# Attention and a low-rank mixer on one core: the first batch's query, key and value handling is reordered

## The chip, the core and the metric

The kernel runs on one core of a Trainium2 chip. Five engines work beside each other, each through its own instructions in order: TensorE (PE in the profile; its weight loads are PEld), VectorE (DVE), ScalarE (ACT), GpSimd (POOL) and SyncE (SP). SyncE only issues transfers; GpSimd issues transfers too, and computes. Sixteen DMA engines carry all transfers. An instruction that waits holds up everything behind it on its engine. The metric is device microseconds from start to end of one execution, and lower is better.

## What is computed

Four batches, eight heads, 768 positions, head dimension 64. First attention with a local window of 96 and 8 global keys, a bias that falls with distance, and a softmax. Then, over the heads' outputs put side by side (512 columns), a low-rank mix over positions and a two-layer feed-forward with residual:

```python
scores = scale * q @ k.T
rel = pos[:, None] - pos[None, :]
keep = (pos[None, :] < 8) | ((rel >= 0) & (rel < 96))
scores = where(keep, scores - slope[h] * dist, -1e9)
x = softmax(scores) @ v            # heads side by side: [4, 768, 512]
u = x + (U @ V applied over positions of x)
out = u + relu(u @ w_ch1) @ w_ch2  # 512 -> 2048 -> 512
```

## The kernel before

**Tiling.** Work goes by pairs of heads: a batch has `NP` = 4 pairs, so pair 0 to 3 are batch 0 and pairs 4 to 15 the others. Positions lie in six blocks of 128. Since the window is below 128, a block of queries needs only its own block of keys and the one before, in which the 8 global keys are put in place of the first positions. Scores are made transposed, keys on partitions: 1408 columns for a head, in three chunks of 512, 512 and 384.

**Steps of a pair i.**
- `load_qk(i)`: two transfers from SyncE's queue, 393 KB each, into staging tiles `qst` and `kst` with three buffers each (L86 to L96). `cast_qk`: a cast of each to 16 bits (L102), on VectorE for pairs 0 and 1, on GpSimd for the others.
- `load_v(i)`: from GpSimd's queue, one transfer a head, with a cast to 16 bits, into one of four buffers `vbuf` (L110). Each row moved is 64 numbers long.
- `st_T(i)`: twelve transposes on TensorE (L223) into two PSUM tiles, then copies to SBUF: the query half of head 0 by ScalarE (L229), keys kT by VectorE (L230), kA, which is the previous block's keys with the global keys put in (L231, L232), and the query half of head 1 by VectorE (L235).
- `st_A(i)`: vA, the same for v: one copy on GpSimd (L241), then the global rows on VectorE (L242).
- Scores: batch 0 uses `st_SE(i, c)`, in which TensorE adds the bias by a matmul of a scaled identity `slI` with a table `rel16` (L258), then the score matmuls (L263, L268), and ScalarE takes the exp straight from PSUM (L281). Later batches use `st_S` (the bias is added by VectorE from a table `relcat`, L294) and `st_E` (exp, L302).
- `st_V(i, hi)`: 11 matmuls a head (L314, L318) whose 65th column is the sum of the weights; VectorE normalises (L323, L325) and GpSimd casts the result to `x16` (L328).
- `st_M1(i)`: six matmuls with U (L336) and a copy of the result, `tmp` (L340). `st_M2(i)`: matmuls with V and an identity (L347, L352) that give `uT`, transposed, copied by VectorE and ScalarE (L358, L360).
- When all four pairs of a batch are through M2, `queue_ff` makes its feed-forward: units of four matmuls `hps` with W1 (L376) and a relu (L380, into `htr`, two buffers), and units of four matmuls with W2 (L389, L395), then the output (L401, L402). `fill(n)` puts n units of the batch before between the steps of later pairs.

**What sets the order.** Batch 0 has no feed-forward work beside it. Its order is written out by hand, within `tc.manual_schedule()`, up to `ordered.close()`: per engine the instructions stand as the code names them, though a scheduler may put instructions of the part behind it between them. In the loop over pairs (L428 on) the first score chunk is followed by the M1 of two pairs ago, the V of the pair before and the casts of pair i + 2; then chunk 1, then `st_T(i + 1)` with the slopes of the next pair's two heads (L162), the next load, M2 of two pairs ago, chunk 2 and `st_A(i)`. W1 is loaded at i = 1, W2 at i = 3, v of pair i + 2 at i = 2 and 3, four transfers for each weight, all from GpSimd's queue with a cast. Behind `ordered.close()` come pairs 4 to 15, where the scheduler chooses each engine's order.

Of the kernel before, what the change touches and what calls it, by code (L numbers as in the profile page):

```python
# [11 lines left out]
FP32 = mybir.dt.float32  # L12
# [8 lines left out]
def kernel(  # L21
# [13 lines left out]
    nc = tc.nc  # L35
    B, H, S, D = q.shape
    NG = int(n_global)
    NL = int(n_local)
    P = 128
    DM = H * D  # L40
    NSB = S // P
# [41 lines left out]
    NVB = 4  # L83
    vbuf = [cst.tile([P, 2, NSB, D + 1], FP16, name=f"v16_{i}") for i in range(NVB)]

    def load_qk(i):  # L86
        b, h0 = i // NP, 2 * (i % NP)
        got = []
        for src, nm in ((q, "qst"), (k, "kst")):
            st = stp.tile([P, 2, NSB, D], FP32, name=nm, tag=nm, bufs=3)  # L90
            nc.sync.dma_start(
                st.rearrange("p h n d -> p h (n d)"),
                src[b, h0:h0 + 2].rearrange("h (p n) d -> p h (n d)", n=NSB),
            )
            got.append(st)
        staged[i] = got  # L96

    def cast_qk(i, eng):
        got = []
        for st, nm in zip(staged.pop(i), ("q16", "k16")):  # L100
            st16 = stp.tile([P, NSB, 2, D], FP16, name=nm, tag=nm, bufs=2)
            eng.tensor_copy(st16.rearrange("p n h d -> p h n d"), st)  # L102
            got.append(st16)
        cast[i] = got

    def load_v(i):
        b, h0 = i // NP, 2 * (i % NP)
        vt = vbuf[i % NVB]
        for hi in range(2):
            nc.gpsimd.dma_start(  # L110
                vt[:, hi, :, 0:D], v[b, h0 + hi].rearrange("(n p) d -> p n d", p=P)
            )
        vts[i] = vt

    NPAIR = B * NP
# [2 lines left out]

    ordered = ExitStack()
    ordered.enter_context(tc.manual_schedule())  # L120
    for i in range(3):
        load_qk(i)


# [4 lines left out]
    def warm(n):  # L129
        wps = ps_oc("warm")  # L130
        for _ in range(n):
            nc.tensor.matmul(wps, zw[:, 0:P], zw, start=True, stop=True)
# [24 lines left out]

    slI = cst.tile([P, H, P], BF16, name="slI")

    def slopes(h0, h1):  # L160
        for h in range(h0, h1):
            nc.vector.tensor_scalar_mul(slI[:, h], ident16, slope[h] / qk_scale)  # L162

    slopes(0, 2)
    for vt in vbuf:
        nc.vector.memset(vt[:, :, :, D:D + 1], 1.0)
    load_v(0)
# [15 lines left out]
    def load_uv():  # L183
        nc.gpsimd.memset(u16, 0.0)
        nc.gpsimd.dma_start(u16[:, :, 0:R], moe_U.rearrange("(c p) r -> p c r", p=P))
        nc.gpsimd.memset(v16w, 0.0)
        nc.gpsimd.dma_start(v16w[0:R], moe_V)
# [10 lines left out]
    def load_w2(c):  # L198
        nc.gpsimd.dma_start(w2_16[:, 4 * c:4 * c + 4], w2v[:, 4 * c:4 * c + 4])
# [4 lines left out]
    def new_batch(b):  # L204
        xs[b] = xp.tile([P, NSB, DM], FP32, name="x_sb", tag="x_sb", bufs=3)
        x16s[b] = xp.tile([P, NSB, DM], FP16, name="x16", tag="x16")
        tmps[b] = xp.tile([P, DM], FP16, name="tmp16", tag="tmp16", bufs=3)
        uTs[b] = xp.tile([P, NDC, S], FP16, name="uT", tag="uT")
# [4 lines left out]
    def st_T(i):  # L213
        stq, stk = cast.pop(i)
        kT = kp.tile([P, S], FP16, name="kT", tag="kT")
        kA = kp.tile([P, NSB - 1, P], FP16, name="kA", tag="kA")
        tps = []
        for st in (stq, stk):

            tp = ps_th("tp", FP16, S)  # L220
            tps.append(tp.rearrange("d (n p) -> d p n", n=NSB))
            for n in range(NSB):
                nc.tensor.matmul(  # L223
                    tp[:, n * P:(n + 1) * P], st[:, n].rearrange("s h d -> s (h d)"), ident16,
                    is_transpose=True, start=(n == 0), stop=(n == NSB - 1),
                )
        tq, tk = tps
        z = qz[i % 2]
        nc.scalar.copy(z[0][0:D].rearrange("d (p n) -> d p n", n=NSB), tq[0:D])  # L229
        nc.vector.tensor_copy(kT.rearrange("d (p n) -> d p n", n=NSB), tk)  # L230
        nc.vector.tensor_copy(kA.rearrange("d n p -> d (n p)"), kT[:, 0:S - P])  # L231
        nc.vector.tensor_copy(  # L232
            kA[:, 1:, 0:NG], kT[:, 0:NG].unsqueeze(1).broadcast_to((P, NSB - 2, NG))
        )
        nc.vector.tensor_copy(z[1][D:P].rearrange("d (p n) -> d p n", n=NSB), tq[D:P])  # L235
        kts[i], kas[i] = kT, kA

    def st_A(i):
        vt = vts[i]
        vA = vap.tile([P, 2, NSB - 1, D + 1], FP16, name="vA", tag="vA")  # L240
        nc.gpsimd.tensor_copy(vA, vt[:, :, 0:NSB - 1])  # L241
        nc.vector.tensor_copy(  # L242
            vA[0:NG, :, 1:],
            vt[0:NG, :, 0:1].broadcast_to((NG, 2, NSB - 2, D + 1)),
        )
        vas[i] = vA
# [27 lines left out]
    def st_SE(i, c):  # L274

        if c == 0:
            for hi in range(2):
                eps[i, hi] = scp.tile([P, W], FP16, name=f"ep{hi}", tag=f"ep{hi}")
        for hi in range(2):
            sc, c0, tot, _ = scores(i, hi, c, True)  # L280
            nc.scalar.activation(  # L281
                eps[i, hi][:, c0:c0 + tot], sc[:, 0:tot], AF.Exp, scale=qk_scale
            )
# [47 lines left out]
    def st_M1(i):  # L331
        b, dc = i // NP, i % NP
        ch = slice(dc * P, (dc + 1) * P)
        tps = ps_th("tmp_ps")
        for n in range(NSB):
            nc.tensor.matmul(  # L336
                tps[:, 0:P], u16[:, n], x16s[b][:, n, ch],
                start=(n == 0), stop=(n == NSB - 1),
            )
        nc.vector.tensor_copy(tmps[b][:, ch], tps[:, 0:P])  # L340

    def st_M2(i):
        b, dc = i // NP, i % NP
        ch = slice(dc * P, (dc + 1) * P)
        for g in range(2):
            ups = ps_th("ups")
            nc.tensor.matmul(  # L347
                ups[:, 0:GT], tmps[b][:, ch], v16w[:, g * GT:(g + 1) * GT],
                start=True, stop=False,
            )  # L350
            for t in range(NTG):
                nc.tensor.matmul(  # L352
                    ups[:, t * P:(t + 1) * P], x16s[b][:, NTG * g + t, ch], ident16,
                    start=False, stop=(t == NTG - 1),
                )
            dst = uTs[b][:, dc, g * GT:(g + 1) * GT]
            if g == 0:
                nc.vector.tensor_copy(dst, ups[:, 0:GT])  # L358
            else:
                nc.scalar.copy(dst, ups[:, 0:GT])  # L360
# [54 lines left out]


    new_batch(0)
    cast_qk(0, nc.vector)
    st_T(0)
    warm(2)  # L420
    cast_qk(1, nc.vector)
    load_qk(3)
    load_v(1)
    load_uv()
    nc.vector.memset(qz[1][0][D:P], 0.0)
    nc.vector.memset(qz[1][1][0:D], 0.0)
    load_v(2)
    for i in range(NP):  # L428
        st_SE(i, 0)
        if i == 0:  # L430
            cast_qk(2, nc.gpsimd)
        if i >= 2:
            st_M1(i - 2)
        else:
            warm(1)
        if i:
            st_V(i - 1, 0)
            st_V(i - 1, 1)
        if i == 0:
            load_v(3)  # L440
        if i:
            cast_qk(i + 2, nc.gpsimd)
        st_SE(i, 1)
        st_T(i + 1)
        if i < 3:
            slopes(2 * i + 2, 2 * i + 4)
        if i:
            load_qk(i + 3)
        if i >= 2:
            st_M2(i - 2)  # L450
        if i == 1:
            for c in range(4):
                load_w1(c)
        st_SE(i, 2)
        st_A(i)
        if i >= 2:
            load_v(i + 2)
        if i == 2:
            table(relcat)
        if i == 3:  # L460
            for c in range(4):
                load_w2(c)
    st_M1(NP - 2)
    st_V(NP - 1, 0)
    st_V(NP - 1, 1)
    st_M2(NP - 2)
    st_M1(NP - 1)
    st_M2(NP - 1)
    ordered.close()
    queue_ff(0, 0)  # L470
    queue_ff(0, 1)

    new_batch(1)
    for i in range(NP, NPAIR):
        b, hp = divmod(i, NP)
        if i + 3 < NPAIR:
            load_qk(i + 3)
        if i + 2 < NPAIR:
            load_v(i + 2)
        st_A(i)  # L480
        for c in range(3):
            st_S(i, c)
            fill(1)
        st_E(i, 0)
        st_E(i, 1)
        if i > NP:
            st_M2(i - 1)
            if hp == 0:
                queue_ff(b - 1, 0)
                queue_ff(b - 1, 1)  # L490
        fill(2)
        if i + 1 < NPAIR:
            if hp == NP - 1:
                new_batch(b + 1)
            st_T(i + 1)
        if i + 2 < NPAIR:
            cast_qk(i + 2, nc.gpsimd)
        fill(3)
        st_V(i, 0)
        fill(2)  # L500
        st_V(i, 1)
        fill(3)
        st_M1(i)
        fill(1)
# [39 lines left out]
```

## Time and profile before

| | us |
|---|---|
| runs of the kernel: lowest, median, highest | 280.97, 282.31, 283.50 |
| the profiled execution, span from first to last instruction | 279.8 |
| its own time beside that span | not given apart from the span; the three runs stand 1.2 to 3.7 above it |
| PE busy | 255.3 (91%) |
| DVE busy | 147.8 (53%) |
| ACT busy | 123.2 (44%) |
| POOL busy | 87.2 (31%) |
| mean granted TensorE clock | 0.963 of full |

The profile's page opens with busy time by engine, and then cuts the span into 40 slices of 7.0 us each, with one digit a slice: the busy share in tenths. Further views of the same trace are lists of instructions in order of time (start, duration, engine, line, operation, tiles, count, and in brackets the idle time before it with what ended it), a table of waits (who waited for whom: total us, times, longest), a table of busy time for chosen stretches, and transfers by queue. The queue called software_dynamic (q0) is GpSimd's, hardware_dynamic (q1) is SyncE's. In the first 70 us GpSimd's queue moved 6.06 MB in 19168 packets, and SyncE's 8.65 MB in 5984.

### The profile page before, as it was taken

To read this page: it belongs to the slowest core of one execution; us is meant where nothing else is said; L and a number is where in the kernel's file an instruction comes from. 1 tells how busy PE (TensorE), PEld (TensorE's weight loads), DVE (VectorE), ACT (ScalarE), POOL (GpSimd) and SP (SyncE) were. 2 spreads that over 40 slices of the span, in tenths; PEclk is the share of its full clock that TensorE was granted. 3 is DMA by queue.
4 is the path that set the end of the run, shared out by engine and by line. 5 is a ranking of instruction groups with operands and counts; after the bars stand their busy time and mean duration, and the time that the engine had idled before them with its cause. 6 is when DMAs were issued, how large, how long until landed. Compare 5 with 4: busy or idle time off the path is not lost.

```text
span 279.8 us, 5080 instructions
## 1 busy us (share of the span) xinstructions
PE 255.3 (91%) x2076; PEld 156.1 (56%) x2076; DVE 147.8 (53%) x301; ACT 123.2 (44%) x209; POOL 87.2 (31%) x129
## 2 busy tenths in 40 slices
PE   7765775899998999799999999999999999999994
PEld 3544554566556655566456655675566555545541
DVE  6766799156666564755957575754574440010011
ACT  2434551565218650668037630856076604604700
POOL 8948688360425124330606042300200010000000
PEclk9779896699999999999999999999999999999999
DMA  6999999992462527170634023000110021001001
GB/s 220 277 281 181 198 233 235 227 239 25 150 105 15 128 63 152 55 127 2 164 79 40 2 43 64 37 2 0 75 41 0 2 76 40 0 37 75 2 37 75
DMA packets 42327, 26.64 MB, mean 95 GB/s; under 512 B 26912, under 2 KB 39232, under 8 KB 42304
## 3 DMA queue, kind: packets, MB, share of 16 engines
q0 software_dynamic: 30144, 7.44, 27.5%
q1 hardware_dynamic: 12160, 18.88, 20.0%
q8 instruction: 16, 0.26, 0.4%
q14 instruction: 7, 0.06, 0.1%
HBM read 27.46 MB, written 6.29 MB: 121 GB/s over the span
## 4 chain that ended last, share of the span: by engine, by line
PE 62%; DVE 8%; ACT 4%; issue 2%; ACTq 0%
PE hps L376 25%; PE cps L395 24%; ACT ep L302 3%; PE tp L223 3%; DVE sp L294 2%; PE sc L268 2%; PE cps L389 2%; PE sc L263 2%; DVE qz L235 2%; DVE kT L230 2%; DVE osb L401 1%; PE tmp_ps L336 1%; PE ob L318 1%; PE ups L352 1%; PE ups L347 1%
## 5 line engine op out<-in xcount | busy, mean ns | idle before, releaser
L376 PE MATMUL hps<-uT,w 128*128 128x384 f16 x512 | 93.4, 328 | 1.3 <-DVE uT L358 1.3
L395 PE MATMUL cps<-w,htr 128*128 128x512 f16 x384 | 91.3, 379 | 0.0
L380 ACT ACTIVATE htr<-hps 128x384 f16<-128x384 f32 x128 | 61.8, 491 | 55.8 <-PE hps L376 55.1
L376 PEld LDWEIGHTS <-w 128*128 128x128 f16 x512 | 48.9, 98 | 30.7 <-issue 3.8
L395 PEld LDWEIGHTS <-htr 128*128 128x128 f16 x384 | 36.1, 98 | 37.4 <-issue 0.4
L302 ACT ACTIVATE ep<-sp 128x1408 f16<-128x1408 f32 x24 | 31.7, 1368 | 39.5 <-DVE sp L294 39.5
L294 DVE SCALAR_TENSOR_TENSOR sp<-sc,relcat 128x512 f32<-128x512 f32 (+1 forms) x72 | 41.8, 637 | 8.6 <-PE sc L268 8.3
L401 DVE TENSOR_TENSOR osb<-cps,x_sb 128x512 f32<-128x512 f32 x24 | 16.6, 690 | 49.6 <-PE cps L395 49.4
L110 POOL DMA_DIRECT2D v<-in_v_dram x32 | 27.3, 857 | 26.1 <-PE ob L318 13.9
L328 POOL CAST x<-x_sb 128x384 f16<-128x384 f32 x32 | 16.4, 514 | 52.5 <-DVE x_sb L325 52.3
L263 PE MATMUL sc<-qz,kT 128*128 128x128 f16 x192 | 30.4, 228 | 1.7 <-DVE qz L235 1.3
L230 DVE COPY kT<-tp 128x768 f16<-128x768 f16 x16 | 15.3, 957 | 28.0 <-PE tp L223 28.0
L268 PE MATMUL sc<-qz,kA 128*128 128x128 f16 x160 | 27.6, 230 | 1.9 <-DVE kA L231 1.3
L102 POOL CAST q<-qst 128x768 f16<-128x768 f32 x14 | 11.6, 830 | 56.8 <-issue 51.5
L268 PEld LDWEIGHTS <-kA 128*128 128x128 f16 x160 | 16.5, 103 | 10.5 <-issue 2.8
L318 PE MATMUL ob<-v,ep 128*128 128x65 f16 x192 | 17.9, 200 | 4.6 <-ACT ep L302 4.4
L263 PEld LDWEIGHTS <-kT 128*128 128x128 f16 x192 | 19.2, 103 | 4.6 <-DVE qz L235 0.9
L318 PEld LDWEIGHTS <-ep 128*128 128x128 f16 x192 | 14.6, 102 | 9.0 <-ACT ep L302 5.4
L281 ACT ACTIVATE ep<-sc 128x512 f16<-128x512 f32 (+1 forms) x24 | 12.6, 562 | 15.3 <-PE sc L268 15.1
L360 ACT CAST uT<-ups 128x384 f16<-128x384 f32 x16 | 7.5, 469 | 26.8 <-PE ups L352 26.8
L325 DVE TENSOR_TENSOR x_sb<-ob,rcp 128x384 f32<-128x384 f32 x32 | 17.7, 553 | 0.6
L314 PE MATMUL ob<-vA,ep 128*128 128x65 f16 x160 | 15.5, 200 | 0.9 <-POOL vA L241 0.5
(60 smaller groups left out, 236.9 us busy)
## 6 DMA issues: line engine op xcount, KB each, us to landing
qst<-in_q_dram SPq DMA_DIRECT2D x16, 384.0 KB, 5.7
kst<-in_k_dram SPq DMA_DIRECT2D x16, 384.0 KB, 6.1
out_dram<-osb SPq DMA_DIRECT2D x24, 256.0 KB, 2.0
w<-in_moe_w_ch_dram POOLq DMA_DIRECT2D x8, 512.0 KB, 11.9
v<-in_v_dram POOLq DMA_DIRECT2D x32, 96.0 KB, 6.2
u<-in_moe_U_dram POOLq DMA_DIRECT2D x1, 48.0 KB, 12.8
v16w<-in_moe_V_dram POOLq DMA_DIRECT2D x1, 48.0 KB, 11.4
```

The source lines that it names most:

```text
L110: nc.gpsimd.dma_start(vt[:, hi, :, 0:D], v[b, h0 + hi].rearrange("(n p) d -> p n d", p=P))
L230: nc.vector.tensor_copy(kT.rearrange("d (p n) -> d p n", n=NSB), tk)
L263: nc.tensor.matmul(sc[:, o:o + P], kT[:, kb * P:(kb + 1) * P], z[:, kb * P:(kb + 1) * P], start=(o == 0 and not on_pe), stop=(o + P == tot),)
L268: nc.tensor.matmul(sc[:, o + P:o + 2 * P], kA[:, kb], z[:, (kb + 1) * P:(kb + 2) * P], start=False, stop=(o + 2 * P == tot),)
L294: nc.vector.scalar_tensor_tensor(out=sps[i][hi][:, c0:c0 + tot], in0=sc[:, 0:tot], scalar=qk_scale / slope[2 * (i % NP) + hi], in1=relf[:, ...
L302: nc.scalar.activation(ep, sps[i][hi], AF.Exp, scale=slope[2 * (i % NP) + hi])
L318: nc.tensor.matmul(ob[:, qi], ep[:, DG[qi]:DG[qi] + P], vt[:, hi, qi], start=(qi == 0), stop=True,)
L325: nc.vector.tensor_tensor(xo, ob[:, :, 0:D], rcp.unsqueeze(2).broadcast_to((P, NSB, D)), ALU.mult)
L376: nc.tensor.matmul(hps[:, 0:GT], w1_16[:, dc, jt * P:(jt + 1) * P], uT[:, dc, ts], start=(dc == 0), stop=(dc == NDC - 1),)
L380: nc.scalar.activation(cell["htr"][:, jt], hps[:, 0:GT], AF.Relu)
L395: nc.tensor.matmul(cps, htr[:, jc, t * P:(t + 1) * P], w2_16[:, jc], start=False, stop=(jc == NJC - 1),)
L401: nc.vector.tensor_tensor(osb, cps, x_sb[:, n], ALU.add)
```

## The change

Only batch 0 and its borders are touched.

- The staging tiles of pairs 0 to 3 become two tiles `early`, which use the two buffers of `htr`. All eight transfers of these pairs are issued at the start. Later pairs have two staging buffers in place of three, and `load_qk` of pairs 4 and 5 is called at i = 0 and 1.
- v of a pair is one transfer.
- Six of the eight slopes are made by ScalarE ahead of the loop, in place of VectorE within it.
- In batch 0 ScalarE copies both query halves.
- In the loop, behind the first score chunk: `st_A(i)`, the casts of pair i + 2, and `st_T(i + 1)`, and then V of the pair before. M1 of two pairs ago stands behind chunk 1, M2 behind chunk 2. The two single warming matmuls are gone.
- `relcat` is made at i = 0 (before: 2). W1 is loaded at i = 2 (before: 1), v of pairs 4 and 5 at the end of i = 3, W2 behind the loop.
- The first score chunk of pair 4, `st_S(NP, 0)`, is put into the hand-written part. One of two copies of `uT` in batch 0 moves from ScalarE to VectorE.

```diff
 def load_qk(i):
+    if b == 0 and i % 2 == 0:
+        early.append(ffp.tile([P, 4, 2, NSB, D], FP32, name="early", tag="htr"))
-    for src, nm in ((q, "qst"), (k, "kst")):
-        st = stp.tile([P, 2, NSB, D], FP32, name=nm, tag=nm, bufs=3)
+    for n, (src, nm) in enumerate(((q, "qst"), (k, "kst"))):
+        if b == 0:
+            st = early[i // 2][:, 2 * (i % 2) + n]
+        else:
+            st = stp.tile([P, 2, NSB, D], FP32, name=nm, tag=nm, bufs=2)
...
 def load_v(i):
-    for hi in range(2):
-        nc.gpsimd.dma_start(
-            vt[:, hi, :, 0:D], v[b, h0 + hi].rearrange("(n p) d -> p n d", p=P)
-        )
+    nc.gpsimd.dma_start(
+        vt.rearrange("p h n d -> p (h n) d")[:, :, 0:D],
+        v[b, h0:h0 + 2].rearrange("h (n p) d -> p (h n) d", p=P),
+    )
...
-for i in range(3):
+for i in range(NP):
     load_qk(i)
...
-def slopes(h0, h1):
-    for h in range(h0, h1):
+for h in range(H):
+    if h < 2:
         nc.vector.tensor_scalar_mul(slI[:, h], ident16, slope[h] / qk_scale)
-slopes(0, 2)
+    else:
+        nc.scalar.mul(slI[:, h], ident16, slope[h] / qk_scale)
...
 def st_T(i):
...
-    nc.vector.tensor_copy(z[1][D:P].rearrange("d (p n) -> d p n", n=NSB), tq[D:P])
+    if i < NP:
+        nc.scalar.copy(z[1][D:P].rearrange("d (p n) -> d p n", n=NSB), tq[D:P])
+    else:
+        nc.vector.tensor_copy(z[1][D:P].rearrange("d (p n) -> d p n", n=NSB), tq[D:P])
...
 def st_M2(i):
...
-        if g == 0:
+        if g == 0 or b == 0:
             nc.vector.tensor_copy(dst, ups[:, 0:GT])
...
 new_batch(0)
+new_batch(1)
 cast_qk(0, nc.vector)
 st_T(0)
 warm(2)
+load_v(1)
 cast_qk(1, nc.vector)
-load_qk(3)
-load_v(1)
-load_uv()
 nc.vector.memset(qz[1][0][D:P], 0.0)
 nc.vector.memset(qz[1][1][0:D], 0.0)
-load_v(2)
 for i in range(NP):
     st_SE(i, 0)
+    st_A(i)
+    cast_qk(i + 2, nc.gpsimd)
+    st_T(i + 1)
     if i == 0:
-        cast_qk(2, nc.gpsimd)
-    if i >= 2:
-        st_M1(i - 2)
-    else:
-        warm(1)
+        load_v(2)
+        table(relcat)
+    if i == 1:
+        load_v(3)
     if i:
         st_V(i - 1, 0)
         st_V(i - 1, 1)
-    if i == 0:
-        load_v(3)
-    if i:
-        cast_qk(i + 2, nc.gpsimd)
     st_SE(i, 1)
-    st_T(i + 1)
-    if i < 3:
-        slopes(2 * i + 2, 2 * i + 4)
-    if i:
-        load_qk(i + 3)
+    if i < 2:
+        load_qk(i + NP)
+    if i == 0:
+        load_uv()
     if i >= 2:
-        st_M2(i - 2)
-    if i == 1:
+        st_M1(i - 2)
+    if i == 2:
         for c in range(4):
             load_w1(c)
     st_SE(i, 2)
-    st_A(i)
     if i >= 2:
-        load_v(i + 2)
-    if i == 2:
-        table(relcat)
+        st_M2(i - 2)
     if i == 3:
-        for c in range(4):
-            load_w2(c)
+        load_v(NP)
+        load_v(NP + 1)
+load_qk(NP + 2)
 st_M1(NP - 2)
 st_V(NP - 1, 0)
 st_V(NP - 1, 1)
+for c in range(4):
+    load_w2(c)
 st_M2(NP - 2)
+st_S(NP, 0)
 st_M1(NP - 1)
 st_M2(NP - 1)
 ordered.close()
...
-new_batch(1)
 for i in range(NP, NPAIR):
...
     for c in range(3):
-        st_S(i, c)
+        if i > NP or c:
+            st_S(i, c)
         fill(1)
```

More of the change, by code (lines that the diff above doesn't have):

```diff
@@ L84 @@
     vbuf = [cst.tile([P, 2, NSB, D + 1], FP16, name=f"v16_{i}") for i in range(NVB)]
+    early = []
     def load_qk(i):
@@ L438 @@
             st_V(i - 1, 1)
+        st_SE(i, 1)
+        if i < 2:
+            load_qk(i + NP)
         if i == 0:
-            load_v(3)
-        if i:
-            cast_qk(i + 2, nc.gpsimd)
-        st_SE(i, 1)
-        st_T(i + 1)
-        if i < 3:
-            slopes(2 * i + 2, 2 * i + 4)
-        if i:
-            load_qk(i + 3)
+            load_uv()
         if i >= 2:
-            st_M2(i - 2)
-        if i == 1:
+            st_M1(i - 2)
+        if i == 2:
             for c in range(4):
```

## The prediction, made before the changed kernel ran

> **What bounds the kernel now.** I read the forty slices first. From about 52 us TensorE is nearly full to the end; before that no engine is, and the DMA row is.
>
> ```profile
> PE   7765775899998999799999999999999999999994
> DMA  6999999992462527170634023000110021001001
> ...
> 42.00:49.00 7.00, 3.81 (x45) 3.02 (x45) 6.38 (x15) 1.25 (x2) 6.11 (x10) 0.65 1.48 235
> 49.00:56.00 7.00, 6.06 (x34) 3.78 (x35) 1.30 (x4) 3.82 (x6) 2.74 (x4) 0.62 1.18 228
> ```
>
> The last two lines are from the table by stretches: us, then busy us of PE, PEld, DVE, ACT, POOL, clock, DMA share, GB/s. The change touches batch 0, so it can move only the moment at which the unbroken run of feed-forward matmuls begins. In TensorE's timeline that is 52.17 us:
>
> ```profile
> 49.71 0.83 PE L336 MATMUL tmp_ps<-x,u 128*128 128x128 f16 x6
> ...
> 52.17 4.50 PE L376 MATMUL hps<-uT,w 128*128 128x384 f16 x20
> ```
>
> M1 of pair 3 runs at 49.71 (its x16 casts ended at 47.2), M2 follows, then L376. After that the rest of the span is TensorE's work, which the change leaves alone. So the forecast is the shift of this point. What held batch 0 up is in the waits of 0 to 66 us, and its GpSimd timeline shows what matters next:
>
> ```profile
> PE sc L258 <- DVE slI L162: 6.1, 3, 2.9
> ...
> 16.39 0.74 POOL L241 COPY vA<-v 128x650 f16<-128x650 f16 x1
> 22.93 2.98 POOL L196 DMA_DIRECT2D w<-in_moe_w_ch_dram  x4
> 31.86 1.65 POOL L110 DMA_DIRECT2D v<-in_v_dram  x2
> 40.66 1.64 POOL L110 DMA_DIRECT2D v<-in_v_dram  x2
> 47.12 0.73 POOL L241 COPY vA<-v 128x650 f16<-128x650 f16 x1
> ```
>
> Three times TensorE waits, 6.1 us in all, until VectorE has done a pair's copies and slopes (L162). W1 is issued at 22.93, pair 4's v (call it v4) at 31.86, and v4's copy to vA runs at 47.12 without a wait: v4 has had 15 us to land.
>
> **Part by part.** *Gains.* The query copy (L235, 4 x 0.96 us) leaves VectorE; ScalarE does it in 0.79 (row L229), and from 7 to 42 us it was busy 16 of 35 us, so it is hidden. The six slopes of L162 (1.4 us on VectorE) go to ScalarE between 2.6 us (ident16 made) and 5.98 us (its first copy); no ACT row has a 128x128 tile; between nothing and the 0.48 of a 128x384 cast they take 0 to 2.9 us and fit; I cost them at nothing. Two warm matmuls (0.6 each) go; nothing to the 1.2 us that the first twenty hps lost at a clock of 0.62 (4.5 us against 0.65 a group of four); I take nothing, since both kernels idle before that point. The relcat table (1.5 us) moves into a VectorE wait. One v transfer per pair: two issues of 0.82 become one, between 0.82 and 1.64; its packets stay (all v packets are in "under 512 B"). I take 0.82.
>
> *The first new wait.* In the order in which the changed kernel's instructions stand on each engine (it shows every edit in place, so I carry no rival that the change fails to do what it says) vA of pair 0 now stands on GpSimd ahead of the casts of pair 2 and the next loads, and its VectorE half (L242) ahead of kT and kA of pair 1, which pair 1's scores need. It waits for v0. In before, v0's second half landed at 15.5 (the wait at 15.57 on GpSimd). SyncE now queues pairs 0 to 3 at once and pairs 4 and 5 as the first ones land: 12 x 393 KB = 4.7 MB by about 9 us, against five pairs by 11.5. At 0.28 MB/us that keeps its queue full until 17.7; in before it paused at 12 and v then moved 779 and 1112 packets in a us. While it is full the v queue gets 167 to 328 packets a us (slices at 9, 10, 11, 16, 18, 19: mean 232). v0 is 1536 packets: 825 by 12 us, 711/232 = 3.1 more, and the 2.6 from packet 1536 (12.9) to landing (15.5): 17.7. Bounds 15.5 (as before) and 17.7; I take 17.0, nearer to the count.
>
> *The walk from there* (durations: vA 0.74, a pair's casts 1.62, x cast 0.5, kT 0.96, kA 0.33, its fix 0.4, a pair's normalising 1.5, u and V with memsets 3.6, W1 3.0):
> - GpSimd: vA0 to 17.75, casts 2 to 19.4, v2 20.2, u/V 23.8, vA1 24.55, casts 3 26.2, v3 27.0.
> - VectorE: vA1 half 24.85, kT 25.8, kA/fix 26.9, normalising 0 28.4. GpSimd: x0 28.95, vA2 29.7, casts 4 31.35.
> - VectorE: kT/kA 3 32.05, normalising 1 33.55. GpSimd: x1 34.1, **W1 issued 34.1 to 37.1** (before: 22.93), vA3 37.85, casts 5 39.5, v6 40.3, casts 6 41.95.
> - VectorE: kT/kA 4 40.2, query copy 41.2, normalising 2 42.7. GpSimd: x2 43.2, **v4 issued 43.2** (before: 31.86), v5, then **vA4 waits for v4**.
>
> Scores of pairs 2 and 3 start at 26.9 and about 34.5, against 25.25 and 33.90: the saved slope waits have paid for v0, no more. TensorE itself is never late in the walk. kA is 0.33 us in quiet and longer beside GpSimd work: 0.90 at 7.61 and
>
> ```profile
> 38.67 2.22 DVE L231 COPY kA<-kT 128x640 f16<-128x640 f16 x1
> ...
> 38.44 0.83 POOL L102 CAST q<-qst 128x768 f16<-128x768 f32 x1
> 39.21 0.82 POOL L102 CAST k<-kst 128x768 f16<-128x768 f32 x1
> 39.98 0.72 POOL L241 COPY vA<-v 128x650 f16<-128x650 f16 x1
> ```
>
> where it ended with the third GpSimd instruction. In the new order kA of pairs 2 to 4 starts inside the casts; I let it end 0.33 after them. (The Trainium skill, "SBUF — State Buffer", "Who interferes with whom", says that the two engines share a port pair which the first holds for its whole instruction: by that one cast, 0.83, is the most it waits. This row shows three. By the rule the sum would stay; by the row up to 1.5 us more a pair.)
>
> *The second new wait, which sets the end.* Behind vA4 on GpSimd stand v7's issue and the x16 casts of pair 3; on VectorE, vA4's half stands ahead of pair 3's last normalising. Without those casts there is no M1, M2 or hps. v4 is behind W1 in one queue, which serves in order: in before v4, issued during W1, landed 10.2 us later, when W1 was through. And W1 shares with q and k of pairs 7 and 8, issued at 38.7 and 41.2, when their buffers come free:
>
> ```profile
> q0 software_dynamic: 203, 0.20, 124.1%
> ...
> q0 software_dynamic: 111, 0.11, 64.4%
> q1 hardware_dynamic: 112, 0.15, 49.8%
> ```
>
> (packets, MB, share, in the us from 30, and from 36 with a q/k pair moving: W1 falls to half.) W1 is 2.1 MB. In before its packets began 2.6 us after issue and took 13.2 us with one q/k pair beside; W2 took 12.3. A second pair (0.79 MB at 0.157 = 5 us at half rate) adds 2.5: 15.2. So 34.1 + 2.6 + 15.2 = 51.9. Then v6 and v4, 3072 packets at 985 a us (the slices at 13 and 21: 1112 and 859) = 3.1, and 1.2 from last packet to landing (v4 in before: 40.85 to 42.06): **v4 lands at 56.2**, 9 us after it was needed in before.
>
> From landing: vA4 0.74, v7 0.82, two casts 1.0 = 2.6; M1 0.5; tmp, which stands behind two score evictions (0.6 each) on VectorE, 4.1; M2 and uT, hps at 5.0. Left over against before: 0.2 of scores and V matmuls, and 1.0 in which V of pair 4 waits for its exp, because score evictions now stand behind tmp. Together 6.2: 56.2 + 6.2 - 52.2 = **+10.2 us**. Span 290.0. The page gives no time of that execution but its span, 279.8; the runs' median is 2.5 above it: 282.3 + 10.2 = 292.5.
>
> (The Trainium skill, "DMA: Bandwidth & Descriptors", "Rules for kernel authors", says to coalesce many small transfers; its section on the anatomy of one DMA gives 2.0 us fixed for each. That speaks for the single v transfer: an estimate from it is 2 us saved for v4, a sum of +8.2. The trace has no row of such a transfer.)
>
> **Bounds.** Low: v0 at 15.5, no kA delay (0.8), W1 unshared (9.8): v4 lands at 48.5, +2.5. High: v0 at 17.7, v issues of 1.64 twice (1.6), W1 at 13.2 + 2.5, kA 1 us more: about 60, +14; and W2, issued only after the x3 casts, whose first chunk one L395 matmul now needs after six hps units: its shortest landing, 7.6, just fits; 2 us of stall make it +16.
>
> **Rivals.**
> 1. *v4 does not sit behind W1* (the queue serves small transfers between). It then lands 3.0 to 6.2 us (rows of v) after 43.2: +0.2 to +3.4; with v0 at 14.4 as its first half did and 3.0, -2.4. For: several chunks of W1 land within a few us of each other. Against: v4's 10.2 us. Same, 0.07.
> 2. *Faster.* If v4 also lands before GpSimd reaches vA4, pair 3's normalising decides: M1 of 2, V and normalising of 3, casts: 46.9, hps at 49.3 and the 1.2 left over: -1.7; with v0 at 14.4, -4.3: 278. It decides from a v4 landing under 43 us, before the walk has it issued. 0.05.
> 3. *W1 nearly unshared*, since pairs 7 and 8 come later: +3 to +7, about 287. 0.14.
> 4. *W2 late too*: +12 to +16, about 296. 0.14.
>
> My forecast (+7 to +12) has 0.60. One per cent, 2.8 us, is about what runs from 280.97 to 283.5 can tell from no change. Range 285 to 298: the three slower cases, whose outer ends it cuts at the low bound and at +16. Faster 0.05, same 0.07, slower 0.88.
>
> **What would show it.** GpSimd idle for over 8 us ahead of the vA copy at about 45, ended by a v transfer; TensorE's M1 of pair 3 at about 59 and hps from 61; W1's issue near 34; pair 1's kT near 18. If vA4 does not wait, or hps starts before 54, I am wrong, and most likely in v0 or in the queue's order.

## The result and the profile after

| | before | after |
|---|---|---|
| runs, us: lowest, median, highest | 280.97, 282.66, 283.50 | 291.35, 292.80, 292.94 |
| after by before, with its 95% interval | | 1.0362 (1.0318 to 1.0407) |
| span of the profiled execution | 279.8 | 291.0 |
| mean granted clock | 0.963 | 0.952 |
| first `hps` group starts at | 52.17 | 63.53 |
| span behind that point | 227.6 | 227.5 |

The changed kernel is 3.6% slower. (The median of before has one run more in it than the one shown earlier. Ratios, here and below, leave aside a single run in a slower state of the chip, 289.4 us in the experiment with v4 ahead of W1.) The last two rows hold the account: everything behind the first `hps` group takes what it took, and all 11.2 us of the span arise before it. TensorE's and the DMA row of the 40 slices (7.3 us each) show where:

```profile
PE   7709656169999899979999999999999999999994
...
DMA  6996799999936171717064801500010001001001
```

There are two holes in TensorE's row that before did not have: the third slice (0) and the eighth (1). DMA is full in both. The table by stretches (us; busy us of PE, PEld, DVE, ACT, POOL; clock, DMA share, GB/s) has the same two places and one more thing:

```profile
14.00:21.00 7.00, 0.18 (x1) 0.10 (x1) 1.95 (x3) 0.00 (x0) 2.74 (x4) 0.74 1.12 203
21.00:28.00 7.00, 6.07 (x58) 4.80 (x58) 4.68 (x7) 3.61 (x6) 6.41 (x9) 0.53 0.71 44
...
49.00:56.00 7.00, 2.97 (x34) 2.51 (x32) 0.85 (x3) 0.00 (x0) 0.00 (x0) 0.74 1.69 226
```

From 14 to 21 us TensorE did 0.18 us of work; from 49 to 56 VectorE 0.85, ScalarE and GpSimd none. Between them, from 21 to 28, the queues moved only 44 GB/s. What the engines waited for is in the table of waits from 0 to 64 us (total us, times, longest):

```profile
DVE vA L252 <- POOL vA L251: 22.3, 5, 8.3
POOL vA L251 <- DMA v<-in_v_dram: 21.4, 2, 12.6
...
PE tmp_ps L346 <- POOL x L338: 8.5, 1, 8.5
PE sc L273 <- DVE kT L237: 7.3, 1, 7.3
```

The three slope waits of before are gone. In their place GpSimd waits twice for v, 21.4 us in all; VectorE waits behind it; and TensorE waits once for kT (7.3) and once for the x16 casts (8.5). GpSimd's timeline gives the two places (lines have moved by some ten: L251 is the copy to vA, L116 v, L203 W1, L206 W2, L338 the x16 cast):

```profile
18.26 0.73 POOL L251 COPY vA<-v 128x650 f16<-128x650 f16 x1 [12.56 <-DMA v<-in_v_dram]
18.93 0.83 POOL L109 CAST q<-early 128x768 f16<-128x768 f32 x1
...
35.76 2.98 POOL L203 DMA_DIRECT2D w<-in_moe_w_ch_dram  x4
...
46.71 2.03 POOL L116 DMA_DIRECT2D v<-in_v_dram  x2
57.58 0.73 POOL L251 COPY vA<-v 128x650 f16<-128x650 f16 x1 [8.84 <-DMA v<-in_v_dram]
58.24 1.01 POOL L116 DMA_DIRECT2D v<-in_v_dram  x1
59.24 1.13 POOL L338 CAST x<-x_sb 128x384 f16<-128x384 f32 x2
```

In brackets is the idle time before an instruction and what ended it. v0 lands at 18.2; the casts of pair 2 stand behind its copy. W1 is issued 12.8 us later than before. v4 is issued at 46.71, behind W1 in the same queue, and lands at 57.5; the x16 casts of pair 3 stand behind its copy. TensorE's timeline takes it from there:

```profile
60.43 0.80 PE L346 MATMUL tmp_ps<-x,u 128*128 128x128 f16 x6 [8.46 <-POOL x L338]
...
63.53 2.24 PE L386 MATMUL hps<-uT,w 128*128 128x384 f16 x8
```

The chain of waits, read in order of time over the first 64 us, names the same two gaps ("issue" is time for which it names no other instruction): 12.54 us with the issue of v0 and v1 ahead and v0's copy and pair 2's casts behind, and 8.81 us with the issue of v4 ahead and its copy behind.

```profile
5.70 12.54 issue
...
35.76 2.84 POOL w L203 x4
...
46.77 1.98 POOL v L116 x2
48.74 8.81 issue
57.58 0.74 POOL vA L251
```

### The profile page after: what moved, and what is told of

The parts are those of the page before. It is cut to its first block, busy times and chain, and to the rows that moved or that the text cites. A ratio compares the mean times of both kernels' runs of the same rounds, so it can differ in the third digit from the quotient of the medians.

```text
span 291.0 us, 5044 instructions
## 1 busy us (share of the span) xinstructions
PE 254.9 (88%) x2073; PEld 156.1 (54%) x2074; DVE 147.3 (51%) x295; ACT 125.3 (43%) x215; POOL 76.7 (26%) x113
## 4 chain that ended last, share of the span: by engine, by line
PE 64%; DVE 14%; issue 11%; POOL 6%; ACT 4%; POOLq 0%; ACTq 0%
PE hps L386 26%; PE cps L405 23%; ACT ep L312 4%; PE tp L230 3%; DVE kT L237 3%; DVE sp L304 2%; PE sc L273 2%; PE sc L278 2%; DVE qz L245 2%; PE cps L399 2%; POOL v L116 2%; DVE vA L252 2%; DVE osb L411 1%; PE tmp_ps L346 1%; DVE kA L238 1%
## 5 line engine op out<-in xcount | busy, mean ns | idle before, releaser
L338 POOL CAST x<-x_sb 128x384 f16<-128x384 f32 x32 | 16.4, 513 | 69.1 <-DVE x_sb L335 68.8
L109 POOL CAST q<-qst 128x768 f16<-128x768 f32 x12 | 10.0, 833 | 64.9 <-issue 56.1
L237 DVE COPY kT<-tp 128x768 f16<-128x768 f16 x16 | 15.2, 952 | 19.5 <-PE tp L230 19.5
L252 DVE COPY vA<-v 8x520 f16<-8x520 f16 x16 | 9.9, 618 | 22.4 <-POOL vA L251 22.3
L357 PE MATMUL ups<-v16w,tmp 128*128 128x384 f16 x32 | 11.6, 363 | 8.5 <-DVE tmp L350 8.5
L251 POOL COPY vA<-v 128x650 f16<-128x650 f16 x16 | 11.8, 737 | 26.1 <-DMA v<-in_v_dram 21.4
L335 DVE TENSOR_TENSOR x_sb<-ob,rcp 128x384 f32<-128x384 f32 x32 | 17.7, 552 | 0.7
```

What stands on the lines that cost most here:

```text
L335: nc.vector.tensor_tensor(xo, ob[:, :, 0:D], rcp.unsqueeze(2).broadcast_to((P, NSB, D)), ALU.mult)
L338: nc.gpsimd.tensor_copy(x16s[b][:, :, h * D:(h + 1) * D], xo)
```

## The experiments

All of them at a glance. "Ratio" is to the kernel before on the same chip, with its 95% interval; the spans are those of the profiled executions, and each kernel's span lies about 1.8 us below that execution's time.

| kernel | ratio | span | `hps` from | span behind it |
|---|---|---|---|---|
| before | 1 | 279.8 | 52.17 | 227.6 |
| after | 1.0362 (1.0318 to 1.0407) | 291.0 | 63.53 | 227.5 |
| after, v4 ahead of W1 | 1.0135 (1.0077 to 1.0192) | 284.3 | 55.59 | 228.7 |
| after, q and k of pairs 4, 5 held | 1.0271 (1.0216 to 1.0326) | 287.8 | 59.83 | 228.0 |
| after, q and k of pairs 7, 8 held | 1.0220 (1.0169 to 1.0271) | 286.4 | 58.41 | 228.0 |
| after, vA behind V | 1.0032 (1.0003 to 1.0061) | 281.7 | 53.79 | 227.9 |
| before, ScalarE parts alone | 0.9936 (0.9907 to 0.9964) | 278.1 | 50.32 | 227.8 |
| before, one v transfer alone | 0.9908 (0.9879 to 0.9938) | 278.8 | 51.35 | 227.5 |
| before, early loading alone | 1.0068 (1.0044 to 1.0093) | 281.1 | 52.76 | 228.3 |
| rebuilt order | 0.9760 (0.9718 to 0.9803) | 273.1 | 46.30 | 226.8 |

The last column runs from 226.8 to 228.7 while the start of `hps` moves by 17 us. In ten kernels the span is that start plus a constant, to within 1.2 us of before's. Each row is one execution, so a difference of a us between two spans is no more than this scatter; against after, the ratios give the same differences as the spans to within a us.

### v4 ahead of W1

Does v4 come late because it stands behind W1 in one queue? Its issue goes ahead of W1's.

```diff
 # after
     if i == 2:
+        load_v(NP)
+        load_v(NP + 1)
         for c in range(4):
             load_w1(c)
...
-    if i == 3:
-        load_v(NP)
-        load_v(NP + 1)
```

> The changed kernel with one edit: v of pairs 4 and 5 is issued at i = 2 ahead of the four W1 transfers, not at the end of i = 3 behind them. Theory (the copy vA of pair 4 waited 8.8 us for v4, which stood in the queue behind W1): that wait goes, the x16 casts of pair 3 come at about 52 instead of 59.2, hps starts at 55 to 57 instead of 63.5, and the time falls by 6.5 to 8.5 us to about 285. Rival (the slow part is the GpSimd and VectorE chain of batch 0 from the late v0 on, and the wait for v4 only fills time that W1 or another step would have taken): 291 to 293, with the wait replaced by one for W1 or for normalising.

Measured: a span of 284.3, 6.7 less than after. GpSimd's timeline:

```profile
37.48 3.00 POOL L203 DMA_DIRECT2D w<-in_moe_w_ch_dram  x4
...
43.79 0.74 POOL L251 COPY vA<-v 128x650 f16<-128x650 f16 x1
```

W1 is issued 1.7 us later than in after, and yet vA of pair 4 is copied 13.8 us earlier and without a wait. v4's place behind W1 cost 6.7 us. It isn't the whole loss: `hps` starts 3.4 us later than in before, with the first wait, for v0, untouched.

### q and k of pairs 4 and 5 held

Is v0 late because SyncE's queue is kept full? A write of two numbers into each staging tile of these pairs, from an engine that comes to it late, holds their transfers back until the first four pairs are in.

```diff
 # after
+            if i == NP:
+                nc.vector.memset(st[:, 0, 0, 0:2], 0.0)
+            elif i == NP + 1:
+                nc.gpsimd.memset(st[:, 0, 0, 0:2], 0.0)
...
+load_qk(NP)
 for i in range(NP):
...
     cast_qk(i + 2, nc.gpsimd)
+    if i == 0:
+        load_qk(NP + 1)
...
-    if i < 2:
-        load_qk(i + NP)
```

> The changed kernel with q and k of pairs 4 and 5 held back to where the kernel before issued them (pair 4 behind the second VectorE casts, pair 5 behind GpSimd's casts of pair 2, each by a write of two elements into its staging tile). Theory (the full SyncE queue delayed v0 by 2.7 us, and this passes down the whole chain): v0's copy begins at about 15.7 instead of 18.26, W1 is issued near 33.2 instead of 35.8, hps starts near 61, the time falls by 2 to 3 us to about 290.3. Rival (v0's delay is absorbed before W1, the queue behind W1 sets the end alone): v0 earlier, but W1's issue at 35 to 36 and 292 to 293.

Measured: a span of 287.8, 3.2 less than after, a little more than expected (2.6 by the ratios). GpSimd's timeline:

```profile
15.04 0.73 POOL L255 COPY vA<-v 128x650 f16<-128x650 f16 x1 [9.35 <-DMA v<-in_v_dram]
...
32.63 2.99 POOL L207 DMA_DIRECT2D w<-in_moe_w_ch_dram  x4
...
54.35 0.73 POOL L255 COPY vA<-v 128x650 f16<-128x650 f16 x1 [9.49 <-DMA v<-in_v_dram]
```

Against after the first copy is 3.22 us earlier, W1's issue 3.13, the second copy 3.23, `hps` 3.70 and the end 3.2. Nothing on the way absorbs it: what is gained at the first wait arrives at the end.

### q and k of pairs 7 and 8 held

How much of the second wait is W1 sharing the DMA engines? The same device, for the pairs whose transfers run beside W1.

```diff
 # after
+            if i in (NP + 3, NP + 4):
+                nc.gpsimd.memset(st[:, 0, 0, 0:2], 0.0)
...
+load_qk(NP + 3)
+load_qk(NP + 4)
 ordered.close()
...
-    if i + 3 < NPAIR:
+    if NP + 1 < i and i + 3 < NPAIR:
         load_qk(i + 3)
```

> The changed kernel with q and k of pairs 7 and 8 held back until W2 has been issued, so that W1 has the DMA engines to itself. Theory (W1's packets moved at half rate while the two pairs were moving, 43.8 to 52.5): W1 is through at 47.5 to 48.5 instead of 52.3, v4 lands near 53 instead of 57.5, the time falls by 4 to 5 us to about 288.3, less what the late pairs 7 and 8 cost later (0 to 1). Rival (W1's own rate, not the sharing, sets it): no change, 292 to 293.

Measured: a span of 286.4, 4.6 less than after. GpSimd's timeline:

```profile
52.45 0.73 POOL L253 COPY vA<-v 128x650 f16<-128x650 f16 x1 [3.64 <-DMA v<-in_v_dram]
```

The copy of pair 4 comes 5.1 us earlier. Rival 3 of the prediction, had the pairs come later by themselves, would have been this case. How the two queues share is in the packets by queue of the changed kernel from 14 to 17 us, and from 44 to 52 (packets, MB, share of 16 engines' time):

```profile
q1 hardware_dynamic: 585, 0.85, 90.8%
q0 software_dynamic: 586, 0.07, 37.4%
...
q0 software_dynamic: 876, 0.88, 64.5%
q1 hardware_dynamic: 873, 1.27, 50.9%
```

While both queues have work they get the same number of packets, whatever a packet holds: v's are 0.12 KB by this count (0.07 MB in 586), W1's 1.0 and q's and k's 1.45. The Trainium skill ("DMA: Bandwidth & Descriptors", "Queues, rings and completion order") says that each DMA engine takes turns between the queues that have work, a packet at a time. These rows agree with the turns: 586 against 585, and 876 against 873. How many of the profile's packets go in one turn they do not show.

### vA behind V

Is it v's lateness that costs, or what stands behind the copy that waits for it? One line moves; no transfer does.

```diff
 # after
     st_SE(i, 0)
-    st_A(i)
     cast_qk(i + 2, nc.gpsimd)
     st_T(i + 1)
...
         st_V(i - 1, 1)
+    st_A(i)
     st_SE(i, 1)
```

> The changed kernel with one edit: st_A(i) stands behind V of the pair before, so behind the casts of pair i + 2 on GpSimd and behind kT and kA of pair i + 1 on VectorE. Theory (the place of st_A made the late v0 hold up casts, kT and the scores): v0 still lands at 18, but pair 1's kT starts near 12, W1 is issued at about 32 instead of 35.8, and v4, now ahead of v6, lands at 51 to 53; the time falls by 4 to 6 us, to about 287.5. Rival (v0 itself is what the chain needs, wherever st_A stands): 291 to 293.

Measured: a span of 281.7, 9.3 less than after, more than expected; the ratio is near before's. GpSimd's timeline:

```profile
10.85 0.82 POOL L109 CAST q<-early 128x768 f16<-128x768 f32 x1 [4.69 <-DMA early<-in_q_dram]
...
18.62 0.73 POOL L251 COPY vA<-v 128x650 f16<-128x650 f16 x1 [4.50 <-DMA v<-in_v_dram]
...
31.84 2.98 POOL L203 DMA_DIRECT2D w<-in_moe_w_ch_dram  x4
...
40.51 3.04 POOL L116 DMA_DIRECT2D v<-in_v_dram  x3
...
49.94 0.73 POOL L251 COPY vA<-v 128x650 f16<-128x650 f16 x1 [5.76 <-DMA v<-in_v_dram]
50.61 0.51 POOL L338 CAST x<-x_sb 128x384 f16<-128x384 f32 x1
```

v0's copy runs at 18.62, a little later than in after (18.26). But the casts of pair 2 now run at 10.85 in place of 18.93. So the place of the copy has a price of its own, with v0 no earlier. W1 goes out 3.9 us earlier, v4 6.2 (the casts of pair 6, 1.7 us, no longer stand ahead of it, and its copy waits 5.76 in place of 8.84), and one of the two x16 casts and the issue of v7 no longer stand behind pair 4's copy: 1.23 us lie between that copy and M1 (51.17), in place of 2.85. Those two parts are what the expectation lacked.

### Before with the ScalarE parts alone

What do the six slopes and the second query copy on ScalarE bring by themselves?

```diff
 # before
-def slopes(h0, h1):
-    for h in range(h0, h1):
+for h in range(H):
+    if h < 2:
         nc.vector.tensor_scalar_mul(slI[:, h], ident16, slope[h] / qk_scale)
-slopes(0, 2)
+    else:
+        nc.scalar.mul(slI[:, h], ident16, slope[h] / qk_scale)
...
+    if i < NP:
+        nc.scalar.copy(z[1][D:P].rearrange("d (p n) -> d p n", n=NSB), tq[D:P])
...
-    if i < 3:
-        slopes(2 * i + 2, 2 * i + 4)
```

> The kernel before with only the two ScalarE edits: six slopes and both query copies of batch 0 on ScalarE. Theory (the 6.1 us in which TensorE waited for slopes were the last link of VectorE's chain behind each transpose, which gets shorter by a query copy of 0.96 and two slopes of 0.3 to 0.8): about 1 us a pair for three pairs, the time falls by 2 to 4 us to about 279.5. Rival (another wait takes the place, for the copies of v or the casts on GpSimd): 0 to 1 us, 282.

Measured: 0.9936 of before, 1.7 us less span; a little under what was expected. The slope waits (6.1 us) are gone, but most of TensorE's saving is spent at vA, above all at pair 0's, which waits for v0. GpSimd's timeline, and the wait that it makes:

```profile
17.43 0.82 POOL L110 DMA_DIRECT2D v<-in_v_dram  x1 [1.96 <-DMA v<-in_v_dram]
18.24 0.74 POOL L244 COPY vA<-v 128x650 f16<-128x650 f16 x1
```

```profile
PE ob L317 <- POOL vA L244: 5.7, 3, 4.1
```

In before GpSimd got past v0 at 15.57; here at 17.43. VectorE's casts free the staging buffers sooner, q of pair 4 is issued at 8.87 in place of 10.64, and SyncE's queue has more to send while v0 is on its way: from 13 to 14 us it moved 144 packets and v 451, in before 27 and 1112. TensorE now waits 5.7 us for vA, 4.1 of them for pair 0's; in before it was 0.5. A faster engine has made a transfer later.

### Before with one v transfer a pair

```diff
 # before
-        for hi in range(2):
-            nc.gpsimd.dma_start(
-                vt[:, hi, :, 0:D], v[b, h0 + hi].rearrange("(n p) d -> p n d", p=P)
-            )
+        nc.gpsimd.dma_start(
+            vt.rearrange("p h n d -> p (h n) d")[:, :, 0:D],
+            v[b, h0:h0 + 2].rearrange("h (n p) d -> p (h n) d", p=P),
+        )
```

> The kernel before with one v transfer a pair. Theory (GpSimd saves an issue of 0.82 us less the longer one, 0.2, sixteen times, and is not the limit): 0 to 1 us faster, about 282. A rule by which each transfer costs 2 us of its own would make it 1 to 2 us faster, since fewer transfers stand ahead of W1 and of v0.

Measured: 0.9908 of before, which is 2.6 us of 282.24 (1.7 to 3.4 by its interval), more than the theory's 0 to 1 and than the rule's 1 to 2. The two profiled executions differ by only 1.0, with `hps` 0.8 us earlier, but this kernel's is the slowest of its eight. The gain is there; where all of it arises is not shown. v0's copy in GpSimd's timeline, at 16.39 in before:

```profile
15.17 0.73 POOL L241 COPY vA<-v 128x650 f16<-128x650 f16 x1 [1.57 <-DMA v<-in_v_dram]
```

### Before with the early loading alone

```diff
 # before
-for i in range(3):
+for i in range(NP):
     load_qk(i)
...
-load_qk(3)
...
-    if i:
-        load_qk(i + 3)
+    if i < 3:
+        load_qk(i + NP)
```

with the `early` tiles and two staging buffers, as in the change.

> The kernel before with q and k of pairs 0 to 3 loaded at once into the same early tiles, pairs 4 and 5 called as early as in the changed kernel, two staging buffers. Theory (a full SyncE queue delays v0 to about 18 here too, but the old order needs v0 only for V of pair 0 at 18.5): vA of pair 0 at 18 to 18.5 instead of 16.4, the time 0 to 1.5 us longer, about 283. Rival (early loading alone costs what e2 gave back): 2.5 to 3.5 us longer, 285.

Measured: 1.0068 of before (1.9 us, between the two expectations), 1.3 us more span. GpSimd's timeline:

```profile
17.99 0.82 POOL L117 DMA_DIRECT2D v<-in_v_dram  x1 [2.87 <-DMA v<-in_v_dram]
18.80 0.74 POOL L248 COPY vA<-v 128x650 f16<-128x650 f16 x1
```

v0 lands 2.4 us later than in before, by loading alone; the end moves only 1.3, in an order that has the casts of pair 2 ahead of that wait (12.63). By the spans the three parts tried in before come to −1.7 − 1.0 + 1.3 = −1.4 us; the change costs +11.2. By the ratios it is −1.8 − 2.6 + 1.9 = −2.5, and +10.2. Either way some 12.6 is left to the new order of the work, by subtraction and not by a run of it alone.

### A rebuilt order

If the two waits and what stands behind them are the whole loss, an order without them keeps the gains. This takes the changed kernel, with its ScalarE parts and single v transfers, holds q and k of pairs 4 and 5 as above, puts vA behind V, and sends the short transfers and W1 into the time in which GpSimd waited.

```diff
 # after
+load_qk(NP)
+load_v(2)
+load_v(3)
+load_uv()
 for i in range(NP):
     st_SE(i, 0)
-    st_A(i)
     cast_qk(i + 2, nc.gpsimd)
+    if i == 0:
+        load_qk(NP + 1)
+        load_w1(0)
+        load_w1(1)
     st_T(i + 1)
...
         st_V(i - 1, 1)
+    st_A(i)
+    if i == 1:
+        load_v(NP)
+    if i == 2:
+        load_v(NP + 1)
+        load_w1(2)
+        load_w1(3)
     st_SE(i, 1)
```

with the old places of these loads taken out.

> The changed kernel with the causes taken away together: q and k of pairs 4 and 5 held back as in e2; GpSimd issues v2, v3, U, V at once, in the time in which it waited for v0, and W1's first two chunks behind the casts of pair 2; st_A of a pair stands behind the V of the pair before, so that casts and transposes no longer wait for v; v4 is issued at i = 1 and v5 at i = 2, ahead of W1's last two chunks. Theory (both waits were put there by the order alone, and the gains of the change were hidden behind them): v0 at about 15, x16 casts of pair 3 at 37 to 40, hps at 40 to 43 instead of 63.5 (before: 52.2), the time 271 to 275, below both kernels. Rival (TensorE and VectorE themselves cannot do batch 0 in less than the 52 us of before): 281 to 283.

Measured: **275.04 us** (274.52 to 275.65), 0.976 of before (0.9718 to 0.9803): faster than both kernels, its slowest run below the fastest of before (280.64). GpSimd's timeline:

```profile
12.97 1.54 POOL L207 DMA_DIRECT2D w<-in_moe_w_ch_dram  x2
14.50 0.74 POOL L255 COPY vA<-v 128x650 f16<-128x650 f16 x1
...
28.09 1.50 POOL L207 DMA_DIRECT2D w<-in_moe_w_ch_dram  x2
...
42.69 1.13 POOL L342 CAST x<-x_sb 128x384 f16<-128x384 f32 x2
```

No copy to vA waits for a transfer any more; pair 3's x16 casts run at 42.69 (59.24 in after) and `hps` starts at 46.30. From 21 to 28 us the queues move 229 GB/s where after moved 44. What each of its edits brings was not taken apart. The casts and `hps` still come some 3 us later than expected, and the time is at the upper end of what was expected. One wait of the old kind is left: at 38.24 TensorE has waited 4.0 us for `tmp` of pair 1, which stands on VectorE behind the VectorE half of pair 3's vA, and GpSimd copies that vA only at 36.44.

## Why the prediction was right, point by point

The forecast was 292.5 us by way of +10.2 on the span; it is 292.8, and +11.2. The mechanism was right; several terms were off, in both directions. That the time is met to 0.3 us is partly luck: the span was put 1.0 too low, and the step from span to time was put at 2.5, since the time of before's profiled execution was not known, where the executions of the experiments have 1.8. The two errors nearly cancel.

| step of the prediction | predicted | measured in after |
|---|---|---|
| v0 has landed | 17.0 | 18.2 |
| kT of pair 1 | about 18 | 19.83 |
| kA of pairs 2 and 3 done | 26.9, 32.05 | 28.87, 33.86 |
| W1 issued | 34.1 | 35.76 |
| v4 issued | 43.2 | 46.71 |
| W1's packets, from first to last | 15.2 | about 14.7 |
| v4 has landed | 56.2 | 57.5 |
| landing to `hps` | 5.0 | 6.0 |
| left over behind `hps` | 1.2 | −0.2 |

**Only the start of `hps` can move.** Shown: the span behind it is constant in ten kernels, to within 1.2 us.

**The first new wait** was at the place named, and the mechanism was the full SyncE queue: holding two pairs back takes 3.2 us off the span. Its size was too small, and the landing fell outside its upper bound of 17.7. Of the three terms two were taken from before's trace, where the queues were not yet so full: 825 packets by 12 us were 598, and 232 packets a us were 196 (586 in 3 us); only the 2.6 from last packet to landing was too long, since by this count v0's packets end at 16.8 and it landed 1.4 later. With equal turns shown, the rate for a short-packet queue is not a mean of slices but half of the packets.

**What the wait holds up** (the casts of pair 2 on GpSimd, kT of pair 1 on VectorE) was named, and moving the copy shows that it is what costs: W1 goes out 3.9 us earlier with v0 no earlier, where an earlier v0 with the copy in place brings 3.1. The prediction costed place and lateness as one. They are two ways to the same gain, and the place alone, over both waits, gives back 9.3 of 11.2 us.

**VectorE beside GpSimd.** The prediction let kA run until 0.33 us after the casts and took 0.3 for the VectorE half of vA. For pairs 2 and 3 it was the other way round. VectorE's timeline, and beside it GpSimd's of the same us:

```profile
19.02 0.88 DVE L252 COPY vA<-v 8x520 f16<-8x520 f16 x1 [8.08 <-POOL vA L251]
...
25.79 1.65 DVE L252 COPY vA<-v 8x520 f16<-8x520 f16 x1 [2.25 <-POOL vA L251]
27.37 0.94 DVE L237 COPY kT<-tp 128x768 f16<-128x768 f16 x1
28.34 0.33 DVE L238 COPY kA<-kT 128x640 f16<-128x640 f16 x1
```

```profile
25.69 0.83 POOL L109 CAST q<-early 128x768 f16<-128x768 f32 x1
26.46 0.82 POOL L109 CAST k<-early 128x768 f16<-128x768 f32 x1
```

The copy of 8 partitions, 0.29 in before, took 0.88, 1.65, 0.89 and 1.65 for pairs 0 to 3. Behind it kA ran in 0.33 for pairs 2 and 3, and in 0.88 and 0.92 for pairs 1 and 4. Net of v0's 1.2, kA of pairs 2 and 3 ended 0.6 to 0.8 later than in the walk. The Trainium skill ("SBUF — State Buffer", "Who interferes with whom") has the engine that comes first hold the shared ports for one whole instruction. The 0.88 fits one cast. The 1.65 does not: it runs from 25.79 to 27.44, through both casts, as 2.22 did in before through three instructions. The measurement decides: when GpSimd's instructions follow one another closely, a VectorE copy beside them may wait for more than one.

**The walk to W1.** Late by 1.7 us: v0's 1.2 and the term above. The issue of a single v transfer, taken at 0.82 between 0.82 and 1.64, measured 1.01 to 1.05.

**The second new wait** was right in place, cause and order. v4 was issued 3.5 us later than predicted, and it made no difference: what counts is when W1, ahead of it in the queue, is through, and W1 was issued 1.7 late and took 0.5 less. Putting v4 ahead of W1 takes the wait away (6.7 us). Equal sharing with pairs 7 and 8 was priced at 5.4 us (15.2 against 9.8); holding them brought the copy 5.1 earlier. Both gains come out of the same wait of 8.84 us, so they should not add; no run tried them together.

**From landing to the end.** A us more to `hps`, of which 0.25 before M1 (1.13 for the two casts, 1.01 for v7) and 0.7 from M1 to `hps` (3.10 against some 2.4). The 1.2 left over was wrong: V of pair 4 and later ones do wait for their exp, 2.1 us in all against 1.4 in before, but other waits are shorter, TensorE is busy 219.3 us behind that point (219.2 in before), and the span behind it did not grow. These two errors nearly cancel, so the span is missed by 1.0, little less than v4's landing (1.3).

**The single v transfer.** The prediction's estimate from the Trainium skill ("DMA: Bandwidth & Descriptors", on the anatomy of one DMA), 2 us saved for v4 and a sum of +8.2, stood against a sum without it of +10.2. The measured +11.2 does not favour it, and in the change nothing of it can be seen, since v4 waits for W1 anyway. The 2.6 us that single transfers bring alone in before are for all sixteen pairs, and do not test a price for v4.

**Rivals.** Rivals 1 and 2 needed v4 early: it was not. Rival 3 appears as an experiment (286.4 of span). Rival 4 did not occur: the table of waits of after has none for W2.

## What to carry to other kernels

When an instruction that waits for a transfer is moved up in an engine's order, price what stands behind it on that engine, not only the lateness of the transfer: here the copy's place was worth 9.3 us with the first of its transfers no earlier. A short, late-issued transfer behind a large one in the same queue lands when the large one is through; send the short one first, and hold back loads that nobody needs yet. Find the one point behind which the profile is unbroken work, and follow only what moves it.

## What the runs showed that was not expected

- The two queues got packets one for one while both were full (586 to 585; 876 to 873). v's queue alone moved 1222 packets in the us from 54, and 196 beside a full SyncE queue: a queue of short packets falls to a sixth of its rate, while SyncE's, which moved 244 in the us from 7 and 220 in the next with v hardly begun, loses much less.
- From 21 to 28 us the DMA queues of the changed kernel moved 44 GB/s, right after an early loading that had kept them full. The rush at the start made v0 late and left the queues idle later, when W1 could have used them.
- Six slopes of 128x128 took ScalarE 1.30 us in all; each takes 0.29, and they overlap.
- A two-number write into a tile, from an engine that comes to it late, is enough to hold a transfer of 393 KB back, and gained 3.2 and 4.6 us.
